# Issuing the loads of the backward phase from GpSimd, spreading a pair's and a group's pieces, and a last loop in two steps

## The chip, the cores and the metric

The kernel runs on one core of one Trainium2 chip. The core has a matrix engine (TensorE, PE in the profile, with its weight loads as PEld), VectorE (DVE), ScalarE (ACT), GpSimd (POOL) and SyncE (SP), which here only issues DMAs. All DMAs run on the core's 16 DMA engines. A DMA that SP or ACT issues goes through a hardware queue, one that POOL issues through a software queue; the profile lists these queues apart. The metric is the time of one execution on the device in microseconds; before and after are compared by the median of several runs.

## The reference

The kernel computes a transformer block whose attention and feed-forward halves stand side by side, and all its gradients:

```
def _A_ref(x, wqkv, wo):                       # attention, 16 heads of 28
    q, k, v = split((x @ wqkv))
    p = softmax(einsum("bhqd,bhkd->bhqk", q, k) * 28 ** -0.5)
    return einsum("bhqk,bhkd->bhqd", p, v) @ wo

def _B_ref(x, w_gate, w_up, w_down):           # SwiGLU, F = 1792
    return (silu(x @ w_gate) * (x @ w_up)) @ w_down

xn = layernorm(x)
out = x + _A_ref(xn, ...) + _B_ref(xn, ...)
outputs: out, and the vjp of it at grad_out for x, wqkv, wo, w_gate, w_up, w_down
```

x is [1, 2048, 448] in bf16. The 2048 rows are 16 tiles of 128.

## The kernel before

There are three stages. The **forward stage** (up to about 655 us of the span) runs attention forward, the feed-forward part forward and its weight gradients, and leaves in DRAM what later stages need: q, k, v and dO by columns (`qT_d`, `kT_d`, `vT_d`, `dOT_d`), the same by rows (`spq_d`, `spk_d`, `spo_d`), and chunks of hidden activations (`hd_d`).

The **backward stage** (about 656 to 1486 us) is one loop over 512 units and a short drain. The 16 heads are 4 groups of 4, a group is 2 pairs of heads, so there are 8 pairs. A unit is one pair, one block of 512 keys and one tile of 128 queries; 8 units make a window, 8 windows a pair, 16 windows a group, 64 windows the loop. In the code k counts the units, `W = k // 8` the windows and `pos = k % 8` the place in a window. A unit does this:

- PE: scores into PSUM (L852), dP into PSUM (L863); ACT: `E = exp(scores)` (L870); DVE: `ds = dP * E` (L881) into one of 8 buffers.
- six of the 8 `ds` tiles of a window are transposed by a DMA that SP issues (L883), the other two by PE (L776) with a copy by DVE or ACT (L783); all go into `dsT`, from which PE makes dq two windows later (L796).
- PE accumulates dK and dV from `ds` and `E` three units later (L749); every two windows ACT copies them out (`dkv_o`, L755), SP transposes them (L762) and POOL stores them (L764).

Beside the units every window carries one job on PE, given by the list `jobs`: windows 1 to 16 a row tile of the output (`y`, 18 chunk matmuls and x), windows 22 to 37, 42 to 49 and 55 to 62 a row tile of one half of the feed-forward part of dx (`dx`, 14 matmuls), windows 18 to 21, 38 to 41 and 51 to 54 a part of the gradient of wqkv (`dwq`); windows 0, 17, 50 and 63 have none. ACT copies a job's result out (`row_o`, L728) and POOL stores it (L730, L732).

What the backward stage reads comes by loads in the order in which the code issues them, on the queue of the issuing engine, which works through its instructions in order and stops at one whose semaphore is not there yet:

- `job_load` (L655) loads a job's chunk `ck` (448 or 576 KB) and, for `y`, a tile `x_c` (112 KB), two windows ahead, at `pos == 0`; three buffers.
- `load_pair` (L545) makes 8 pieces of 128 KB for the next pair: q and k in rows 0 to 63, dO and v in rows 64 to 127 of the tiles `qT` and `kT`, each in two halves of columns. They wait in the list `pload`.
- `load_group` (L558) makes 6 pieces of 256 KB for the next group (`v_sp`, `vT`, `O_sp`), in the list `gload`.
- `load_w` (L532) makes 7 pieces of a weight of 1568 KB or 2 of `wq`, in `wload`.

At `pos == 4` of each window the first 2 of `pload`, 1 of `gload` and 2 of `wload` are issued. All loads but that of `wd` are issued by SP, in one queue with the transposes. The first pair and the first group are loaded at the end of the forward stage.

The **last stage** (from 1494 us) is a loop over the 16 row tiles: PE sums dx through the projections (L957, L959), ACT copies it with a row sum (`g_sb`, `s1`, L963), DVE takes a product sum (`junk`, `s2`, L966), then `bb` (L970) and `cc` (L972); ACT makes `t1` (L975), DVE `t2` (L977), POOL adds the residual gradient (`dx`, L980) and SP stores it (L981).

Of the kernel before, what the change touches and what calls it, by code (L numbers as in the profile page):

```python
# [10 lines left out]
ALU = mybir.AluOpType  # L11
AX = mybir.AxisListType
FP32 = mybir.dt.float32
BF16 = mybir.dt.bfloat16
# [4 lines left out]
D = 448  # L19
# [3 lines left out]
G = 4  # L23
HP = 32
P = 128
NT = S // P
NFC = F // P
# [10 lines left out]
def kernel(  # L38
# [19 lines left out]
    pe, act, dve, pool, sp = nc.tensor, nc.scalar, nc.vector, nc.gpsimd, nc.sync  # L58
    ctx.enter_context(tc.manual_schedule())
    x_d = A_x.rearrange("b (t p) d -> p (b t) d", p=P)  # L60
    dy_d = grad_out.rearrange("b (t p) d -> p (b t) d", p=P)
    out0_d = out_0.rearrange("b (t p) d -> p (b t) d", p=P)
    out1_d = out_1.rearrange("b (t p) d -> p (b t) d", p=P)
# [9 lines left out]
    hd_d = dram.tile([NT, P, G + 3 * NFC, P], BF16, name="hd_d")  # L73
# [14 lines left out]
    xn_sp = const.tile([P, NT, DP], BF16, name="xn_sp")  # L88
# [39 lines left out]
    for b in (2, 3):  # L128
# [10 lines left out]
        out=r_ones[:], in_=ident_f[:].rearrange("p (a b) -> p a b", b=HP)[:, :, 28:30],  # L139
# [291 lines left out]
    for fc in range(NFC):  # L431
        nxt = dW_items(fc)
# [99 lines left out]
    def load_w(nm, parts):  # L532

        t = wp.tile([P, NFC, D], BF16, name="W")
        src = {"wd": B_w_down.rearrange("(fc p) d -> p fc d", p=P), "wg": wT_d[0], "wu": wT_d[1], "wq": wqT_d}[nm]
        n = 3 * G if nm == "wq" else NFC
        wtile[nm] = t
        step = n // parts
        q = pool if nm == "wd" else sp
        out = [lambda i=i: q.dma_start(out=t[:, i:i + step, :], in_=src[:, i:i + step, :])  # L540
               for i in range(0, n, step)]
        return out

# [2 lines left out]
    def load_pair(pr, parts):  # L546

        g, r = pr // 2, 64 * (pr % 2)
        q = qkp.tile([P, S], BF16, name="qT")
        k = qkp.tile([P, S], BF16, name="kT")  # L550
        qd[pr] = (q, k)
        n = S // parts
        return [lambda i=i, dst=dst, r0=r0, src=src: sp.dma_start(
                    out=dst[r0:r0 + 64, i:i + n], in_=src[g, r:r + 64, i:i + n])
                for r0, srcs in ((0, (qT_d, kT_d)), (64, (dOT_d, vT_d)))
                for dst, src in zip((q, k), srcs) for i in range(0, S, n)]

    def load_group(g, parts, kpool):  # L558

        spt[g] = [qkp.tile([P, NT, P], BF16, name="v_sp"), kpool.tile([P, S], BF16, name="vT"),  # L560
                  qkp.tile([P, NT, P], BF16, name="O_sp")]
        spt[g][1] = spt[g][1][:].rearrange("p (t c) -> p t c", c=P)
        n = NT // parts
        return [lambda i=i, t=t, src=src: sp.dma_start(
                    out=t[:, i:i + n, :].rearrange("p t c -> p (t c)"), in_=src[g, :, i * P:(i + n) * P])
                for t, src in zip(spt[g], (spq_d, spk_d, spo_d)) for i in range(0, NT, n)]

# [20 lines left out]
    for i, (g, qc, kt) in enumerate(steps):  # L588
# [25 lines left out]
        if i in (6, 8, 10, 12):  # L614
            j = i // 2 - 3
# [39 lines left out]
    def job_load(i):  # L655
        if i >= len(jobs) or jobs[i] is None:
            return
        j = jobs[i]
        if j[0] == "y":
            t = ckp.tile([P, NFC + G, P], BF16, name="ck")  # L660
            sp.dma_start(out=t[:], in_=hd_d[j[1], :, :G + NFC, :])
            x = ckp.tile([P, D], BF16, name="x_c")
            sp.dma_start(out=x[:], in_=x_d[:, j[1], :])
            chunk[i] = (t, x)
        elif j[0] == "dx":
            t = ckp.tile([P, NFC + G, P], BF16, name="ck")
            sp.dma_start(out=t[:, :NFC], in_=hd_d[j[2], :, G + NFC * (1 + j[1]):G + NFC * (2 + j[1]), :])
            chunk[i] = t

    def dwq_mms(g, c, ps):  # L670
# [160 lines left out]
    for k in range(N + 2 * UW):  # L831
        W, pos = k // UW, k % UW
        if k < N:
            pr, kc, w, qi = units[k]
            if k % 64 == 3 and pr + 1 < NPR:
                pload.extend(load_pair(pr + 1, 2))
            if k % 128 == 3 and pr + 2 < NPR:
                gload.extend(load_group(pr // 2 + 1, 2, vp if pr // 2 % 2 else ksp))
            if pos == 0:
                job_load(W + 2)  # L840
            if pos == 4:
                if W == len(jobs) - 1:
                    wload.extend(load_w("wq", 2))
                for lst, n in ((pload, 2), (gload, 1), (wload, 2)):
                    for f in lst[:n]:
                        f()
                    del lst[:n]
            q, kv = qd[pr]
            qt = 8 * w + qi
            s_ps = ps_sd.tile([P, 2, 512], FP32, name="sd")  # L850
            for j in range(2):
                pe.matmul(s_ps[:, j, :], lhsT=q[HP * j:HP * j + HP, qt * P:(qt + 1) * P],  # L852
                          rhs=kv[HP * j:HP * j + HP, kc * 512:(kc + 1) * 512],
                          start=True, stop=True, tile_position=(HP * j, 0))
        late_tr = pos == 0 and 1 <= W <= NW
        if 1 <= k <= N:
            pr, kc, w, qi = units[k - 1]
            q, kv = qd[pr]
            qt = 8 * w + qi
            d_ps = ps_sd.tile([P, 2, 512], FP32, name="sd")  # L860
            for j in range(2):
                r = 64 + HP * j
                pe.matmul(d_ps[:, j, :], lhsT=q[r:r + HP, qt * P:(qt + 1) * P],  # L863
                          rhs=kv[r:r + HP, kc * 512:(kc + 1) * 512],
                          start=True, stop=True, tile_position=(r, 0))
        if late_tr:
            pe_transpose(W - 1, TQ[1])
        if k < N:
            E[k] = ework.tile([P, 2, 512], BF16, name="E")
            act.activation(out=E[k][:], in_=s_ps[:], func=ACT.Exp, scale=SCALE)  # L870
        if late_tr:
            tr_out(act)
        job = jobs[W] if W < len(jobs) else None
        if pos == 6 and 2 <= W <= NW + 1:
            dq_out(W - 2)
        if 1 <= k <= N:
            if qi == 0:
                st[("dsT", (k - 1) // UW)] = twin.tile([P, 2, 4, UW * P], BF16, name="dsT")
            dsT = st[("dsT", (k - 1) // UW)]
            DS[k - 1] = dsw.tile([P, 2, 512], BF16, name="ds")  # L880
            dve.tensor_tensor(out=DS[k - 1][:], in0=d_ps[:], in1=E[k - 1][:], op=ALU.mult)  # L881
            if qi not in TQ:
                sp.dma_start_transpose(out=dsT[:, :, :, qi * P:(qi + 1) * P].rearrange("p j c q -> p (j c) q"),  # L883
                                       in_=DS[k - 1][:].rearrange("p j c -> p (j c)"))
        while sp_later:
            sp_later.pop(0)()

        if pos == 1:
            if 3 <= k < N + 3:
                acc_mm(k - 3)  # L890
            if job:
                st["aux"] = ps_x.tile([P, 512], FP32, name="aux")
                fillers = job_mms(W, st["aux"])
        if 1 <= pos < 5 and job:
            n = -(-len(fillers) // (5 - pos))
            for f in fillers[:n]:
                f()
            fillers = fillers[n:]
        if k == N + UW + 5:
            for c in range(4):  # L900
                if c % 2 == 0:
                    g_t = ps_sd.tile([P, 2, 512], FP32, name="sd")
                last_dwq.append((g_t[:, c % 2, :], dwq_mms(3, c, g_t[:, c % 2, :])))
            for _, m in last_dwq:
                for f in m[0][:12]:
                    f()
        if pos == 5 and 2 <= W <= NW + 1:
            dq_mm(W - 2, 0)
            dq_mm(W - 2, 1)
        if pos != 1 and 3 <= k < N + 3:  # L910
            acc_mm(k - 3)
        if pos == 4 and job:
            job_out(W, st["aux"])
        if pos == 6 and W < NW:
            pe_transpose(W, TQ[0])
            tr_out(dve)
# [5 lines left out]
    with ExitStack() as fin:  # L922
# [20 lines left out]
        for part in range(2):  # L943
            for c, (ps, m) in enumerate(last_dwq):
                for f in m[part][12 * (1 - part):]:
                    f()
                if part == 1:
                    dwq_out(3, c, ps)
        wq = wtile["wq"]
        for t in range(NT):  # L950
            if t % 2 == 0:
                load_c(t // 2 + 3, act)
# [5 lines left out]
            for n in range(3 * G):  # L958
# [14 lines left out]
                                     op0=ALU.mult, op1=ALU.mult)  # L973
            t1 = wk.tile([P, D], FP32, name="t1")
            act.activation(out=t1[:], in_=g_ps, func=ACT.Identity, scale=rstd[:, t:t + 1], bias=bb[:, 0:1])  # L975
            t2 = wk.tile([P, D], FP32, name="t2")
            dve.scalar_tensor_tensor(out=t2[:], in0=xn_sp[:, t, :D], scalar=cc[:, 0:1], in1=t1[:],  # L977
                                     op0=ALU.mult, op1=ALU.add)
            dx = wk.tile([P, D], BF16, name="dx")
            pool.tensor_tensor(out=dx[:], in0=t2[:], in1=dy_t[:, t, :], op=ALU.add)  # L980
            sp.dma_start(out=out1_d[:, t, :], in_=dx[:])  # L981
    cst.close()


# [28 lines left out]
```

## Time and profile before

| what | value |
|---|---|
| median of 3 runs (lowest, highest) | 1548.89 us (1547.53, 1555.15) |
| profiled execution, its span | 1549.43 us, 1547.7 us |
| busy PE, DVE, ACT, POOL | 1412.8, 1099.4, 1187.9, 396.1 us |
| backward stage, 656 to 1486 us: PE, DVE, ACT, POOL | 756.6, 678.7, 621.1, 110.1 us of 830.0 |
| its DMA rate, mean | 199 GB/s |
| transposes of `ds`: number, issue by SP (least, median, most) | 384, 1.231, 1.293, 5.001 us |

The span is the time from the first to the last instruction of the profiled execution; the execution itself was 1.8 us longer. A DMA's row on an issuing engine is the time that the issue takes; the data land later. Views used below: the page, the sums by window of time, the timeline of one engine in a stretch of time, and the chain of waits, which goes back from the last instruction by what released each.

### The profile page before, as it was taken

Reading aid. Unit: us, or ns where it says so; the run is one execution under the profiler, and the core shown is the slowest. Engines: PE = TensorE matmul, PEld = TensorE weight load, DVE = VectorE, ACT = ScalarE, POOL = GpSimd, SP = SyncE. Lnnn points to the kernel's source line nnn. Section 1 sums busy time; section 2 is a strip of 40 time slices with the busy share of each in tenths; the row PEclk is TensorE's granted clock in tenths of the full one; section 3 lists DMA queues with packets and bytes.
Section 4 is the critical chain, followed back from the end, with each engine's and each line's share of the span. In section 5 each row is a group of like instructions: output and inputs, shape, how many; then the busy total and the mean of one; then the engine's idle time right before and its main releaser. Section 6 shows DMA issues by size and latency. Waiting matters only on the chain.

```text
span 1547.7 us, 32024 instructions
## 1 busy us (share of the span) xinstructions
PE 1412.8 (91%) x12176; PEld 597.7 (39%) x12176; DVE 1099.4 (71%) x1421; ACT 1187.9 (77%) x1333; POOL 396.1 (26%) x664
## 2 busy tenths in 40 slices
PE   6899999999999989988988988989999889999987
PEld 3333333333333333433433444433335333543353
DVE  7654555656666657476877877878878789888935
ACT  6898988888788878676767867878778778888724
POOL 4341433343435355310110111111102101111033
PEclk9999999999999999999999999999999999999999
DMA  9985758767978689799999999999999999999994
GB/s 225 189 174 113 157 101 173 161 142 141 179 154 164 148 173 215 159 205 200 214 204 206 196 199 205 198 200 198 207 197 197 200 192 197 174 192 215 188 274 142
DMA packets 682106, 285.12 MB, mean 184 GB/s; under 512 B 637136, under 2 KB 650464, under 8 KB 681952
## 3 DMA queue, kind: packets, MB, share of 16 engines
q1 hardware_dynamic: 652016, 210.03, 74.6%
q0 software_dynamic: 25968, 64.53, 16.8%
q10 hardware_dynamic: 3968, 8.52, 1.6%
q8 instruction: 95, 1.56, 0.4%
q14 instruction: 59, 0.48, 0.1%
HBM read 67.34 MB, written 63.44 MB: 85 GB/s over the span
## 4 chain that ended last, share of the span: by engine, by line
PE 56%; DMA 13%; ACT 13%; DVE 8%; issue 6%; SPq 1%; POOL 1%; ACTq 0%; DVEq 0%; POOLq 0%
DMA dsT<-ds 9%; PE f_ps L357 7%; PE sd L852 6%; PE s_ps L600 6%; PE f_ps L383 6%; ACT E L870 5%; PE aux L719 4%; PE acc L749 4%; PE aux L796 4%; PE aux L776 4%; PE o_ps L582 4%; ACT eT L605 4%; DVE ds L881 3%; ACT dsT L783 3%; PE aux L713 3%
## 5 line engine op out<-in xcount | busy, mean ns | idle before, releaser
L881 DVE TENSOR_TENSOR ds<-sd,E 128x1024 bf16<-128x1024 f32 x512 | 611.4, 1220 | 137.5 <-DMA dsT<-ds 52.6
L870 ACT ACTIVATE E<-sd 128x1024 bf16<-128x1024 f32 x512 | 516.9, 1024 | 178.4 <-PE sd L863 140.2
L605 ACT ACTIVATE eT<-s_ps 128x1024 bf16<-128x1024 f32 x512 | 495.8, 1026 | 93.1 <-PE s_ps L600 89.6
L852 PE MATMUL sd<-kT,qT 32*128 32x512 bf16 x1024 | 201.8, 390 | 24.7 <-DVE ds L881 22.3
L863 PE MATMUL sd<-kT,qT 32*128 32x512 bf16 x1024 | 202.6, 389 | 23.6 <-ACT E L870 22.7
L749 PE MATMUL acc<-ds,v_sp 128*32 128x512 bf16 x1024 | 204.6, 395 | 0.7 <-DVE ds L881 0.7
L749 PE MATMUL acc<-E,O_sp 128*32 128x512 bf16 x1024 | 204.3, 395 | 0.2 <-ACT dkv_o L755 0.2
L600 PE MATMUL s_ps<-qT,kT 32*128 32x512 bf16 x1024 | 148.0, 386 | 7.8 <-ACT eT L605 5.6
L422 POOL DMA_DIRECT2D hd_d<-fT x168 | 126.9, 769 | 15.5 <-DVE fT L407 6.8
L383 PE MATMUL f_ps<-xnT,wgu 128*128 128x512 bf16 x448 | 118.8, 383 | 4.9 <-DVE w_sb L409 4.7
L764 POOL DMA_DIRECT2D dqkv_d<-dkv_o x64 | 39.3, 619 | 289.1 <-ACT dkv_o L755 287.3
L719 PE MATMUL aux<-W,ck 128*128 128x448 bf16 x448 | 108.4, 359 | 3.4
L852 PEld LDWEIGHTS <-qT 32*128 32x128 bf16 x1024 | 51.3, 91 | 154.1 <-issue 145.5
L582 PE MATMUL o_ps<-eT,v_sp 128*32 128x512 bf16 x1024 | 103.4, 394 | 0.6
L357 PE MATMUL f_ps<-xn_sp,f_sp 128*128 128x448 bf16 x448 | 99.1, 354 | 0.0
L749 PEld LDWEIGHTS <-O_sp 128*32 128x32 bf16 x1024 | 50.4, 94 | 113.4 <-issue 103.4
L600 PEld LDWEIGHTS <-kT 32*128 32x128 bf16 x1024 | 40.7, 91 | 137.7 <-issue 132.7
L776 PE MATMUL aux<-ident_bf,ds 128*128 128x128 bf16 x1024 | 79.4, 221 | 11.2 <-DVE dq_acc L808 5.8
L863 PEld LDWEIGHTS <-qT 32*128 32x128 bf16 x1024 | 65.4, 91 | 62.1 <-issue 58.2
L357 PEld LDWEIGHTS <-f_sp 128*128 128x128 bf16 x672 | 58.2, 98 | 77.4 <-issue 23.4
L776 PEld LDWEIGHTS <-ds 128*128 128x128 bf16 x1024 | 61.8, 98 | 39.8 <-issue 39.4
L395 DVE SCALAR_TENSOR_TENSOR g<-t_sb,f_ps 128x512 f32<-128x512 f32 x56 | 38.4, 686 | 53.3 <-ACT t_sb L393 53.2
(133 smaller groups left out, 1766.5 us busy)
## 6 DMA issues: line engine op xcount, KB each, us to landing
hd_d<-fT POOLq DMA_DIRECT2D x168, 128.0 KB, 4.4
ck<-hd_d SPq DMA_DIRECT2D x32, 448.0 KB, 4.4
ck<-hd_d SPq DMA_DIRECT2D x16, 576.0 KB, 5.1
dsT<-ds SPq DMA_TRANSPOSE x384, 4.2
dqkv_d<-dkv_o POOLq DMA_DIRECT2D x64, 64.0 KB, 3.8
dq_c<-dqkv_d ACTq DMA_DIRECT2D x5, 768.0 KB, 6.5
W<-wT_d SPq DMA_DIRECT2D x14, 224.0 KB, 3.6
out_dram<-dw_o POOLq DMA_DIRECT2D x28, 96.0 KB, 4.0
```

The source lines that it names most:

```text
L357: pe.matmul(acc[:, :D], lhsT=src[:, 12 * (t // 4) + 4 * wi + t % 4, :], rhs=rhs[:, t, :D], start=(t == 0), stop=(t == NT - 1))
L383: pe.matmul(st[name][:], lhsT=w(c), rhs=src[:, tsl, c, :], start=(c == 0), stop=(c == 3))
L582: pe.matmul(o_ps[HP * hh:HP * (hh + 1), :], lhsT=v[:, kt, HP * hh:HP * (hh + 1)], rhs=e[hh // 2][:, hh % 2, :], start=(kt == 0), stop=(kt ...
L600: pe.matmul(s_ps[:, j, :], lhsT=kT[r:r + HP, kt * P:(kt + 1) * P], rhs=qT[r:r + HP, qc * 512:(qc + 1) * 512], start=True, stop=True, tile_ ...
L605: act.activation(out=e[:], in_=s_ps[:], func=ACT.Exp, scale=SCALE)
L719: return [lambda n=n: pe.matmul(ps[:, :D], lhsT=t[:, n, :], rhs=w[:, n, :], start=(n == 0), stop=(n == NFC - 1)) for n in range(NFC)]
L749: pe.matmul(acc[r:r + HP, :], lhsT=src[:, qt, 64 * hp + HP * j:64 * hp + HP * j + HP], rhs=m[:, j, :], start=(qt == 0), stop=(qt == NT - 1 ...
L776: pe.transpose(ps[:, i, :], ds[:, i // 4, (i % 4) * P:(i % 4 + 1) * P], ident_bf[:])
L852: pe.matmul(s_ps[:, j, :], lhsT=q[HP * j:HP * j + HP, qt * P:(qt + 1) * P], rhs=kv[HP * j:HP * j + HP, kc * 512:(kc + 1) * 512], start=Tru ...
L863: pe.matmul(d_ps[:, j, :], lhsT=q[r:r + HP, qt * P:(qt + 1) * P], rhs=kv[r:r + HP, kc * 512:(kc + 1) * 512], start=True, stop=True, tile_p ...
L870: act.activation(out=E[k][:], in_=s_ps[:], func=ACT.Exp, scale=SCALE)
L881: dve.tensor_tensor(out=DS[k - 1][:], in0=d_ps[:], in1=E[k - 1][:], op=ALU.mult)
```

## The change

All loads of `load_w`, `load_pair`, `load_group` and `job_load` are issued by POOL instead of SP (the `wd` load was already). SP keeps the DMA transposes and, in the last stage, its loads and stores there. Of a pair's 8 pieces one is issued in each window instead of two, first halves of the columns first; of a group's 6 pieces one in every second window. In the last loop the second half of a tile's work (`t2`, `dx`, the store) is put behind the first half of the next tile, and the add of the last three tiles moves from POOL to DVE.

```
@@ load_w
-        q = pool if nm == "wd" else sp
-        out = [lambda i=i: q.dma_start(out=t[:, i:i + step, :], in_=src[:, i:i + step, :])
+        out = [lambda i=i: pool.dma_start(out=t[:, i:i + step, :], in_=src[:, i:i + step, :])
@@ load_pair
-        return [lambda i=i, dst=dst, r0=r0, src=src: sp.dma_start(
+        return [lambda i=i, dst=dst, r0=r0, src=src: pool.dma_start(
@@ load_group
-        return [lambda i=i, t=t, src=src: sp.dma_start(
+        return [lambda i=i, t=t, src=src: pool.dma_start(
@@ job_load
-            sp.dma_start(out=t[:], in_=hd_d[j[1], :, :G + NFC, :])
+            pool.dma_start(out=t[:], in_=hd_d[j[1], :, :G + NFC, :])
-            sp.dma_start(out=x[:], in_=x_d[:, j[1], :])
+            pool.dma_start(out=x[:], in_=x_d[:, j[1], :])
-            sp.dma_start(out=t[:, :NFC], in_=hd_d[j[2], :, G + NFC * (1 + j[1]):G + NFC * (2 + j[1]), :])
+            pool.dma_start(out=t[:, :NFC], in_=hd_d[j[2], :, G + NFC * (1 + j[1]):G + NFC * (2 + j[1]), :])
@@ loop over units
             if k % 64 == 3 and pr + 1 < NPR:
-                pload.extend(load_pair(pr + 1, 2))
+                nxt = load_pair(pr + 1, 2)
+                pload.extend(nxt[0::2] + nxt[1::2])
-                for lst, n in ((pload, 2), (gload, 1), (wload, 2)):
+                for lst, n in ((pload, 1), (gload, W % 2), (wload, 2)):
@@ last loop
+        def finish(t, t1, cc):
+            t2 = wk.tile([P, D], FP32, name="t2")
+            dve.scalar_tensor_tensor(out=t2[:], in0=xn_sp[:, t, :D], scalar=cc[:, 0:1], in1=t1[:],
+                                     op0=ALU.mult, op1=ALU.add)
+            dx = wk.tile([P, D], BF16, name="dx")
+            add = pool if t < NT - 3 else dve
+            add.tensor_tensor(out=dx[:], in0=t2[:], in1=dy_t[:, t, :], op=ALU.add)
+            sp.dma_start(out=out1_d[:, t, :], in_=dx[:])
...
             act.activation(out=t1[:], in_=g_ps, func=ACT.Identity, scale=rstd[:, t:t + 1], bias=bb[:, 0:1])
-            t2 = wk.tile([P, D], FP32, name="t2")
-            dve.scalar_tensor_tensor(out=t2[:], in0=xn_sp[:, t, :D], scalar=cc[:, 0:1], in1=t1[:],
-                                     op0=ALU.mult, op1=ALU.add)
-            dx = wk.tile([P, D], BF16, name="dx")
-            pool.tensor_tensor(out=dx[:], in0=t2[:], in1=dy_t[:, t, :], op=ALU.add)
-            sp.dma_start(out=out1_d[:, t, :], in_=dx[:])
+            if t > 0:
+                finish(t - 1, *held)
+            held = (t1, cc)
+        finish(NT - 1, *held)
```

## The prediction

> **What bounds the kernel now.** I started with the page: its span, the chain that ended last and the costliest group. The profiled execution took 1549.43 us, 0.5 above the median of 1548.89, for a span of 1547.7 us; the sum below is made against it.
>
> ```profile
> span 1547.7 us, 32024 instructions
> ...
> DMA dsT<-ds 9%; PE f_ps L357 7%; PE sd L852 6%; PE s_ps L600 6%; PE f_ps L383 6%; ACT E L870 5%; PE aux L719 4%; PE acc L749 4%; PE aux L796 4%; PE aux L776 4%; PE o_ps L582 4%; ACT eT L605 4%; DVE ds L881 3%; ACT dsT L783 3%; PE aux L713 3%
> ...
> L881 DVE TENSOR_TENSOR ds<-sd,E 128x1024 bf16<-128x1024 f32 x512 | 611.4, 1220 | 137.5 <-DMA dsT<-ds 52.6 <-PE sd L863 51.5 <-ACT E L870 13.5
> ```
>
> The longest single item of the chain is a transfer, the transposes of `ds`, and DVE, which makes `ds`, loses 52.6 us waiting for them: `ds` has 8 buffers, so its tile k needs the transpose of tile k-8 to be done. All this is in the backward phase. Its 512 `ds` instructions run from 658.0 to 1473.4 us, 815.4 us; I cut that into its 64 windows of 8 units and asked for L881 window by window (columns: stretch, length, DVE busy, TensorE clock, DMA share, GB/s).
>
> ```profile
> core 0: us, DVE busy (x), PEclk, DMA share, GB/s
> 714.60:729.90 15.30, 9.53 (x9) 1.00 1.05 203
> 729.90:741.70 11.80, 9.41 (x9) 1.00 1.15 237
> ...
> 896.50:913.70 17.20, 9.64 (x9) 0.90 1.01 199
> 1090.50:1102.40 11.90, 9.67 (x10) 1.00 1.10 224
> 1130.60:1145.00 14.40, 9.65 (x10) 0.86 1.02 195
> ...
> 1366.30:1378.10 11.80, 9.62 (x10) 1.00 1.08 195
> ```
>
> The work of a window is the same, yet its length goes from 11.8 to 17.2 us. After 1366 us, where the last pair's loads are over, all are 11.8 to 12.1. The long ones move fewer GB/s than the short ones, so bytes alone don't stretch them. Then SP's own rows inside the window of 14.4 us (start, us, line):
>
> ```profile
> 1128.21 1.26 SPq L883 DMA_TRANSPOSE dsT<-ds  x1
> 1129.53 1.22 SPq L553 DMA_DIRECT2D kT<-vT_d  x2
> 1130.79 0.58 SPq L564 DMA_DIRECT2D vT<-spk_d  x1
> 1131.48 9.64 SPq L883 DMA_TRANSPOSE dsT<-ds  x6
> 1141.20 1.23 SPq L762 DMA_TRANSPOSE dkv_sp<-dkv_o  x1
> 1142.49 0.58 SPq L564 DMA_DIRECT2D O_sp<-spo_d  x1
> 1143.17 6.76 SPq L883 DMA_TRANSPOSE dsT<-ds  x5
> ```
>
> SP issues back to back for 21.7 us with 0.05 us between rows. **The bound of the stretched windows is SP's issue time.** From the records of all SP rows between 658.0 and 1473.4: 428 transposes 652.7 us (mean 1.525), 152 loads 95.2 us (0.63 each), 580 gaps of 0.06: 783 of 815 us. The median transpose is 1.29 us; the excess of the mean, (1.525 - 1.29) x 428 = 101 us, is 0.66 us for each load, for transposes that stand right behind loads in the ring are issued slowly (up to 2.8 us). So a window's SP time is 6.75 transposes x 1.35 = 9.1 us, plus 1.35 us for each load (0.63 + 0.06 + 0.66). Test on groups: windows 1 to 16 have 3.2 loads each, 13.4 us by this, and measure 13.5; windows 18 to 21 have 3.75, 14.2, and measure 14.4; windows 55 to 62 have 1.1, 10.6, and measure 11.9, the pitch that the compute engines set.
>
> **The change part by part.**
>
> *Loads from SP to POOL.* SP loses all 152 loads and keeps 9.1 us of transposes a window plus whatever surcharge s loads in another queue still put on them. If s stays 0.66, a `y` window (3.4 loads after the change) costs SP 9.1 + 2.2 = 11.3 and the others (2.1 loads) 10.5, both below the compute pitch. The pitch comes from windows with little SP lag: 11.91 for `dx` (mean of 55 to 62), 12.0 for `dwq` (51 to 54), 10.8 and 10.9 for those without a job, and 12.2 for `y` (mean of 5 to 7 and 13 to 16). Gains: `y` 216.0 - 16 x 12.2 = 20.8; `dwq` 155.5 - 144.0 = 11.5; first `dx` 203.6 - 190.6 = 13.0; `dx` 42 to 49 99.7 - 95.3 = 4.4; sum 49.7. I leave 4 us of it for `y` windows in which loads and transposes still meet (windows 6 and 7 took 12.5 and 12.7), and take 46. Bounds: all `y` at 11.9 gives 54; nothing gained if s rises (rivals).
>
> *POOL's side.* 152 issues more. A load has no POOL row of this shape; the stores L732 (0.57) and L764 (0.62), and 1.10 for the 1568 KB `W` load of L540, bound one by 0.5 and 1.1 us; I take 0.6, near the plain stores: 3.4 x 0.6 + 1.2 = 3.3 us of a 12 us window, where POOL's busy time is now 0.6 to 3.0. POOL is in order, so a load waits behind a `row_o` store that waits for ACT (up to 15.6 us) or a `dkv_o` one (18.4). That costs nothing while chunk i is asked for two windows (24 us) ahead, landing in 4.4 to 5.1, and pair pieces at least three units ahead. If that cover went, PE would wait for its next chunk or `qT` by what is late, some us per pair, 7 times. The first chunk loses most cover: SP issues it at 657.3, POOL only after its stores end at 662.5; landing 5.5 us later is 668.0, and the first `ck` weights load at 669.4. Zero, with 0 to 3 us for the range. The 7 loads of the first pair and group (578 to 606 us) join a POOL with waits of its own in a stretch that PE bounds: zero.
>
> *Pieces spread.* One pair piece a window instead of two in four of eight, a group piece every second window: no instruction more or less. It flattens the load, and its worth is inside the 46. The last piece of a pair is issued in the eighth window, about 4 units (6 us) before the next pair, and needed later still, since it holds the second half of the columns; landing 3.0 to 3.5 us covers it.
>
> *Tail in two steps.* In the last loop a tile's pieces chain: ACT `t1`, DVE `t2`, POOL `dx`, and the next `bb` on DVE ends only with `dx`:
>
> ```profile
> 1540.51 0.69 DVE L977 SCALAR_TENSOR_TENSOR t<-xn_sp,cc,t 128x448 f32<-128x448 bf16 x1 [0.85 <-ACT t L975]
> 1541.66 0.67 DVE L970 SCALAR_TENSOR_TENSOR bb<-s,rstd 128x1 f32<-128x1 f32 x1
> ...
> 1541.28 1.03 POOL L980 TENSOR_TENSOR dx<-t,dy_t 128x448 bf16<-128x448 f32 x1 [1.70 <-DVE t L977]
> ```
>
> `bb` takes 0.67 where its first two took 0.16, and the tile's period is 2.73 us against 2.65 for PE alone (the pitch of the first tiles). Moving `t2` and `dx` behind the next tile's `cc` breaks the ring: PE ends at 1494.1 + 16 x 2.65 = 1536.5 instead of 1537.8. Then g_sb 0.75, junk 0.7, bb and cc 0.3, `t2` of tile 14 0.69, its add on DVE, `t2` of tile 15 0.69, its add. No DVE add of this shape is in the trace; L881's 1.19 ns per element gives 0.53, L508's 1.35 gives 0.61; I take 0.6. That ends at 1540.9; now POOL's last `dx` ends at 1545.0. Gain 4.1, say 4, bounds 1 (if a wait for loads holds PE's pitch) and 5.
>
> The Trainium skill has the reason for the slow `bb`: "SBUF — State Buffer", section "Who interferes with whom", says that a DVE instruction with two SBUF inputs shuts out, or is shut out by, a GpSimd instruction that reads SBUF. The trace agrees, 0.67 against 0.16 us; by the rule the `t2` moved next to another `dx` could be blocked for up to 1.0 us too, which PE's 2.65 us would hide.
>
> **Sum.** 1549.4 - 46 - 4 = 1499 us.
>
> **The rivals.**
> 1. *Transposes still held in `y` windows.* If s is 1.2, a `y` window is 9.1 + 3.4 x 1.2 = 13.2, 1 us over the pitch, others 11.6, under it: 1499 + 16 = 1515. For it: a `y` window would move 2.9 MB (transposes 1.77, chunk 0.59, the rest 0.55), 244 GB/s at 11.9 us, over any full window's (237). Against: 224 and 237 at full pitch.
> 2. *The DMA engines bind, whoever issues.* Then 162.4 MB at the mean of 199 GB/s is 816 us as now, and the tail alone is left: 1545. The skill says so in general: "DMA: Bandwidth & Descriptors", section "Issuing engines are not separate DMA queues", has it that several issuing engines save only the sequencer's time, usually small beside the DMA. Here 783 of 815 us of SP's time is not small. Against it too: 224 GB/s and more in windows of 12 us.
> 3. *Slower: POOL's packets in a queue of their own cut into the transposes.* With SP bound everywhere the windows sum to 591 + 145 x s us (54 for 16 `y` windows, 91 for 44 others); from s = 1.57 that beats the gain of the tail and it is slower; at 1.8 it is 852, and 1582 us in all. For it: from 606 to 617 us POOL issued some 10 stores, and a transpose of `fT` beside them took 4.25 us where the median is 1.46, the next on SP 3.48 instead of 1.47. Against: these 4.8 us are 0.5 a store, below 0.66.
> 4. *The change doesn't do what it says*, loads late behind POOL's waits: the cover above, some 5 us on a gain of 50; its chance is counted with the forecast, whose range holds it.
>
> **Chances.** Forecast 0.70 (own range 1487 to 1508), first rival 0.14, second 0.07, third 0.09. The range 1487 to 1530 takes in the forecast and the first rival. A measurement of this kernel tells 0.5% (7.7 us) from no change: faster 0.84, same 0.07, slower 0.09.
>
> **What would show it.** Right: SP rows with idle time between transposes, no DVE wait for `dsT<-ds` near 52.6 us, `y` windows at 12.2 to 12.4, `dwq` and `dx` at 12, clock 1.00 throughout, POOL's load rows near 0.6 us; in the tail `bb` at 0.16 and a period of 2.65. Wrong: mean transpose issue above 1.7 us, windows of 14 us without SP lag, or PE waiting for `ck`, `qT` or `kT`.

## The result and the profile after

| kernel | median of its runs, us (lowest, highest) | ratio to before, 95% interval |
|---|---|---|
| before | 1548.21 (1545.40, 1555.15) | |
| after | 1615.97 (1606.34, 1622.29) | 1.0425 [1.0353, 1.0498] |

The change makes the kernel 4.2% slower; 1499 us had been forecast. Medians here and below are of all runs of a kernel, ratios of those within 1.5% of its fastest run. The profiled execution of the changed kernel took 1610.19 us. First the page of the changed kernel: span, chain by line, and the group of `ds`.

```profile
span 1608.4 us, 32018 instructions
...
DMA dsT<-ds 17%; PE f_ps L357 7%; PE f_ps L383 6%; PE s_ps L599 6%; PE sd L852 5%; ACT eT L604 4%; PE acc L748 4%; PE aux L795 4%; PE aux L718 4%; ACT E L870 4%; PE o_ps L581 3%; PE aux L775 3%; PE aux L712 2%; DVE ds L881 2%; PE sd L969 2%
L881 DVE TENSOR_TENSOR ds<-sd,E 128x1024 bf16<-128x1024 f32 x512 | 610.5, 1219 | 197.9 <-DMA dsT<-ds 126.4
```

DVE's own work is what it was (610.5 us), but it now waits 126.4 us for transposes of `ds`, 73.8 more than before, and their share of the chain went from 9 to 17%. The 512 units run from 658.7 to 1538.3 us: 879.6 us against 815.4, so 64.2 us are lost there. The first `ds` comes 0.7 us later than before, and from the end of the last to the end of the span it is 70.1 us where it was 74.3, so 4.2 us come back there; the span grew by 60.7. The cut of L881 by windows (stretch, length, DVE busy, TensorE clock, DMA share, GB/s):

```profile
core 0: us, DVE busy (x), PEclk, DMA share, GB/s
694.00:706.50 12.50, 9.52 (x9) 1.00 0.96 191
732.50:753.00 20.50, 9.39 (x9) 0.83 1.14 169
790.60:809.70 19.10, 9.60 (x10) 0.82 1.15 190
...
931.60:953.40 21.80, 9.50 (x8) 0.92 1.21 157
1102.40:1114.20 11.80, 9.61 (x10) 1.00 1.12 183
```

The loss isn't spread evenly. 46 of the 64 windows last 12.17 us on average, close to the pitch that was forecast (769.4 / 64 = 12.0). The other 18 are longer than 14 us and take 319.8 us, 17.8 each; before there were 13 such windows with 193.2 us. The windows of 20.5 and 21.8 us move 169 and 157 GB/s at a DMA share of 1.14 and 1.21, the one of 11.8 us 183 at 1.12: the DMA engines are as busy with packets and move less.

How a long window comes about is seen on POOL and SP just ahead of the one of 21.8 us (start, us, engine, line; idle time ahead in brackets):

```profile
921.95 1.20 POOL L763 DMA_DIRECT2D dqkv_d<-dkv_o  x2 [8.90 <-ACT dkv_o L754]
923.13 0.54 POOL L552 DMA_DIRECT2D qT<-dOT_d  x1
923.67 1.10 POOL L539 DMA_DIRECT2D W<-wT_d  x2
924.76 1.07 POOL L698 COPY dwq_z<-dwq_raw 128x56 bf16<-128x56 bf16 x6
926.12 0.72 POOL L699 DMA_DIRECT2D out_dram<-dwq_z  x1 [0.30 <-POOL dwq_z L698]
926.73 0.65 POOL L552 DMA_DIRECT2D kT<-vT_d  x1
927.27 0.65 POOL L563 DMA_DIRECT2D v_sp<-spq_d  x1
927.83 1.15 POOL L539 DMA_DIRECT2D W<-wT_d  x2
```

POOL stood 8.90 us before a store that waits for ACT. Everything queued behind it, two pieces of a pair, one of a group and four of weights, then leaves with three stores in 7 us. SP in the same time:

```profile
918.73 1.28 SPq L817 DMA_TRANSPOSE dq_sp<-dq_o  x1
920.10 7.73 SPq L883 DMA_TRANSPOSE dsT<-ds  x4
927.92 1.65 SPq L761 DMA_TRANSPOSE dkv_sp<-dkv_o  x1
929.66 3.07 SPq L883 DMA_TRANSPOSE dsT<-ds  x1
```

Four transposes take SP 7.73 us, where four of 1.29 would take 5.2; those issued at 916 to 918 us landed 3.3 us later, those issued from 922.9 to 929.7 landed 8.6 to 10.0 us later. Over the whole stage the transposes of `ds` land 5.47 us after their issue (4.30 before), 63 of them later than 8 us (none before). SP's 428 transposes take 1.871 us each against 1.525, so SP, rid of 95 us of loads, needs 148 us more for transposes; its gaps of over 0.3 us sum to 36 of the 880 us.

The longest window is the first, 22.8 us where it was 11.8. POOL issues nine loads in it from 663.00 to 668.08 us, right behind its stores; the first two transposes land 16.0 and 15.5 us after their issue, and DVE stands:

```profile
681.48 3.49 DVE L881 TENSOR_TENSOR ds<-sd,E 128x1024 bf16<-128x1024 f32 x3 [11.63 <-DMA dsT<-ds]
```

In the last stage `bb` takes 0.15 us and the period is 2.65 us, (1602.97 - 1592.38) / 4:

```profile
1592.38 0.15 DVE L980 SCALAR_TENSOR_TENSOR bb<-s,rstd 128x1 f32<-128x1 f32 x1
...
1602.97 0.15 DVE L980 SCALAR_TENSOR_TENSOR bb<-s,rstd 128x1 f32<-128x1 f32 x1
```

### The profile page after: what moved, and what is told of

Same layout as the page of the kernel before. It is cut to its first block, busy times and chain, and to the rows that moved or that the text cites. A ratio compares the mean times of both kernels' runs of the same rounds, so it can differ in the third digit from the quotient of the medians.

```text
span 1608.4 us, 32018 instructions
## 1 busy us (share of the span) xinstructions
PE 1430.6 (89%) x12176; PEld 598.7 (37%) x12176; DVE 1094.6 (68%) x1424; ACT 1189.1 (74%) x1333; POOL 479.4 (30%) x822
## 4 chain that ended last, share of the span: by engine, by line
PE 55%; DMA 21%; ACT 11%; DVE 7%; issue 6%; POOL 1%; SPq 0%; DVEq 0%; ACTq 0%; POOLq 0%
DMA dsT<-ds 17%; PE f_ps L357 7%; PE f_ps L383 6%; PE s_ps L599 6%; PE sd L852 5%; ACT eT L604 4%; PE acc L748 4%; PE aux L795 4%; PE aux L718 4%; ACT E L870 4%; PE o_ps L581 3%; PE aux L775 3%; PE aux L712 2%; DVE ds L881 2%; PE sd L969 2%
## 5 line engine op out<-in xcount | busy, mean ns | idle before, releaser
L881 DVE TENSOR_TENSOR ds<-sd,E 128x1024 bf16<-128x1024 f32 x512 | 610.5, 1219 | 197.9 <-DMA dsT<-ds 126.4
L852 PE MATMUL sd<-kT,qT 32*128 32x512 bf16 x1024 | 206.9, 400 | 83.8 <-DVE ds L881 81.8
L863 PE MATMUL sd<-kT,qT 32*128 32x512 bf16 x1024 | 207.6, 398 | 22.0 <-ACT E L870 21.3
L748 PE MATMUL acc<-ds,v_sp 128*32 128x512 bf16 x1024 | 208.7, 403 | 0.7 <-DVE ds L881 0.7
L748 PE MATMUL acc<-E,O_sp 128*32 128x512 bf16 x1024 | 208.5, 403 | 0.2 <-ACT dkv_o L754 0.2
L795 PE MATMUL aux<-dsT,vT 128*32 128x512 bf16 x1024 | 81.9, 428 | 0.4
```

The costliest lines, as they stand in the source:

```text
L748: pe.matmul(acc[r:r + HP, :], lhsT=src[:, qt, 64 * hp + HP * j:64 * hp + HP * j + HP], rhs=m[:, j, :], start=(qt == 0), stop=(qt == NT - 1 ...
L795: pe.matmul(ps[r:r + HP, :], lhsT=Ks[:, kc * 4 + kt, 64 * hp + HP * j:64 * hp + HP * j + HP], rhs=dsT[:, j, kt, s_ * 512:(s_ + 1) * 512], ...
```

## The experiments

All twelve kernels are timed against the kernel before. "Harm" below is the time above that of the kernel with every load on SP and the two other parts of the change (the second experiment, 1540.07 us).

### The last loop alone

The kernel before with nothing but `finish` and `held` from the diff.

> The kernel before with the last loop in two steps alone. Every theory of the loads leaves this run alone: the last stage should lose the 2.73 us ring and end about 4 us earlier, 1544 to 1545 us against 1548.5, ratio 0.997. If the changed kernel's loss had its place in the last loop, it would be slower than before.

1545.43 us (1538.82 to 1553.01), ratio 0.9982 [0.9963, 1.0001]; the 64 windows sum to 816.0 us (815.4 before). From the last `ds` to the end of the span it is 71.1 us instead of 74.3, a gain of some 3 us; the interval of the ratio just takes in no change.

### Everything but the queue

```
-        out = [lambda i=i: pool.dma_start(out=t[:, i:i + step, :], in_=src[:, i:i + step, :])
+        q = pool if nm == "wd" else sp
+        out = [lambda i=i: q.dma_start(out=t[:, i:i + step, :], in_=src[:, i:i + step, :])
...
-            pool.dma_start(out=t[:], in_=hd_d[j[1], :, :G + NFC, :])
+            sp.dma_start(out=t[:], in_=hd_d[j[1], :, :G + NFC, :])
```

The same in `load_pair`, `load_group` and for the other loads of `job_load`.

> All loads stay on SP, pieces spread over the windows, last loop in two steps. Theory 1 (copies in a queue other than that of the transposes cut into them packet by packet) and theory 2 (only POOL's software queue does) both expect no loss here: SP stays at its 9.1 us of transposes plus 1.35 us a load, but no window has more than 4 loads, so 1525 to 1543 us. Theory 3 (the new order of the pieces, or pieces that come late, is what costs) expects this slow as well, 1580 us or more.

1540.07 us (1536.30 to 1544.61), ratio 0.9947 [0.9929, 0.9965]. So the spread of the pieces is worth some 5 us on SP (windows 808.6 instead of 816.0), and the move to POOL alone costs 1615.97 - 1540.07 = 76 us.

### The same loads from ACT's hardware queue

The changed kernel with `act` in place of `pool` in the five loads.

> The changed kernel with the loads issued by ACT, in ACT's hardware queue, instead of POOL. Theory 1 (any second queue cuts into the transposes): as slow as the changed kernel, 1590 us or more, transposes with issues of 3 to 8 us and landings above 8 us. Theory 2 (POOL's software queue alone): SP is free and nothing cuts into the transposes, 1500 to 1520 us, median landing of the transposes 4 us or less; ACT pays 0.4 us a load.

1549.80 us (1544.92 to 1558.74), ratio 1.0012 [0.9988, 1.0036]: the time of neither theory, but the transposes tell "any second queue" from "POOL's queue". From the waits of DVE in the stage (us, times, longest):

```profile
DVE ds L882 <- PE sd L864: 86.5, 198, 0.9
...
DVE ds L882 <- DMA dsT<-ds: 1.4, 1, 1.4
```

and from the DMA issues of its page (KB, median us to landing):

```profile
ck<-hd_d ACTq DMA_DIRECT2D x32, 448.0 KB, 4.1
...
dsT<-ds SPq DMA_TRANSPOSE x384, 4.4
```

The wait for transposes is gone (1.4 us), SP stands idle for 117 us, and a transpose takes SP 1.545 us: the surcharge is (1.545 - 1.29) x 428 / 152 = 0.72 us a load, about the 0.66 that the forecast used. What the forecast said of SP is true of a second hardware queue. The time doesn't fall, for ACT now issues the loads between its own instructions: of the `dx` windows, 55 to 59, in each of which ACT issues a chunk, take 12.52 or 12.79 us where they took 11.78 or 12.05, and window 61, in which it issues nothing, takes 11.78 as before. `ds` waits for dP (86.5 us, 51.5 before) instead of transposes.

### POOL without the spreading

```
-                pload.extend(nxt[0::2] + nxt[1::2])
+                pload.extend(load_pair(pr + 1, 2))
...
-                for lst, n in ((pload, 1), (gload, W % 2), (wload, 2)):
+                for lst, n in ((pload, 2), (gload, 1), (wload, 2)):
```

> The changed kernel with the pieces as before, two of a pair and one of a group in a window. Theories 1 and 2: as slow as the changed kernel or slower, since two pieces and a chunk then meet in one window, 1605 to 1640 us. Theory 3 (the spreading costs): back to 1550 us or less.

1620.81 us (1610.91 to 1634.22), ratio 1.0473 [1.0427, 1.0520]: 4.8 us above the changed kernel, but the runs overlap, and in its profile the windows sum to 873.2 us against 879.6. With the loads on POOL no worth of the spreading is shown; it isn't what does the harm.

### Half of the loads on POOL

First only `ck` and `x_c` on POOL, then only pairs, groups and weights, the rest on SP.

> The changed kernel with only the chunks ck and x_c (64 loads, 25 MB) on POOL; pairs, groups and weights (88 loads, 17 MB) on SP. Theory 1 (a load in POOL's software queue reaches the 16 DMA engines at different times and breaks the step that the transposes need, for as long as its bytes last): loss over e2_sp_spread by bytes, 60% of 76 us, about 1585 us, transposes with landings over 8 us beside chunks alone. Theory 2 (the number of loads in the queue counts): 42%, about 1572. Theory 3 (only all of it together saturates something, POOL or its ring): near e2, 1530 to 1545.

> The other half: pairs, groups and weights on POOL, the chunks on SP. Theory 1: 40% of the loss, about 1570 us, and windows 55 to 62, which have no such loads, at 11.9 us. Theory 2: 58%, about 1584. Theory 3: 1530 to 1545.

Chunks alone: 1564.66 us (1562.25 to 1568.40), ratio 1.0101 [1.0070, 1.0132], harm 24.6 us. The others alone: 1551.18 us (1539.60 to 1564.33), ratio 1.0012 [0.9980, 1.0044], harm 11.1 us (8.5 without the two longest of its ten runs); its one profile is of an execution 11.6 us above that median, so nothing is read from it. Both expectations by bytes or by number missed, and in the same direction: 24.6 + 11.1 = 36 us at the most, not 76. More than half of the harm is there only when both kinds come from POOL.

### Fewer loads, or none, in SP's ring

Two tests of the forecast's other half, that SP's issue time is the bound and that windows fall to a pitch of 12 when it is lifted. In the first the loads are larger and fewer (105 instead of 152: a pair in 4 pieces, a group in 3, a weight in 2), all on SP; in the second the chunk loads are left out.

> e2_sp_spread with larger and fewer loads on SP: a pair in 4 pieces of 256 KB, a group in 3 of 512 KB, a weight in 2 of 784 KB, one at a time in alternate windows; 105 loads instead of 152, the same bytes. If SP's issue time bounds the stretched windows and a load costs it 0.69 us itself, 47 x 0.69 = 32 us of SP time are saved in the 40 windows that have them: 1515 to 1530 us. If the bytes in the ring are what costs (the 0.66 us of surcharge and more), no faster than e2: 1538 to 1548.

> e2_sp_spread in which the first chunk ck and x_c are used by all jobs: 62 loads (24 MB) are left out, all matmuls stay. If SP's issue time bounded the stretched windows, SP falls to 9.1 + 1.4 x 1.35 = 11.0 us a window, under the pitch of the compute engines, and the 64 windows take what the prediction took for them, 765 to 775 us instead of 809: 1497 to 1507 us. If that pitch was wrong (the compute engines need more than 12 us), windows stay above 780 us and the time above 1512.

Fewer loads: 1532.39 us (1528.24 to 1534.80), ratio 0.9894 [0.9871, 0.9917], 7.7 us better than the same with 152 loads, but 2.4 us above the range that was expected for it. Without chunk loads: 1507.42 us (1504.53 to 1509.44), ratio 0.9735 [0.9709, 0.9762], 0.4 us above its range, and no window is longer than 13.7 us. A `y` and a `dx` window of the latter, in the columns used above:

```profile
747.70:760.20 12.50, 9.61 (x10) 1.00 0.85 169
1088.80:1100.60 11.80, 9.61 (x10) 1.00 1.12 198
```

The waits of its DVE:

```profile
DVE ds L888 <- PE sd L870: 61.9, 149, 1.7
...
DVE ds L888 <- DMA dsT<-ds: 0.5, 1, 0.5
```

With 62 loads fewer on SP its transposes no longer hold anything up (0.5 us), and the windows sum to 777.3 (765 to 775 were expected). That fits the bound as it was named, and the pitch, but for `y`: 12.5 instead of 12.2. The run takes 25 MB off the DMA engines too, though, so by itself it doesn't tell SP's issue time from their bytes; the copies below do.

### Copies in place of transposes

Two theories for the harm. One: a transpose needs all 16 DMA engines in step, and POOL's loads reach the engines at different times and break the step. The other: POOL's queue holds up whatever SP issues. For them the transposes of `ds` are replaced by plain copies of the same size:

```
-                sp.dma_start_transpose(out=dsT[:, :, :, qi * P:(qi + 1) * P].rearrange("p j c q -> p (j c) q"),
-                                       in_=DS[k - 1][:].rearrange("p j c -> p (j c)"))
+                sp.dma_start(out=dsT[:, :, :, qi * P:(qi + 1) * P],
+                             in_=DS[k - 1][:].rearrange("p j (c q) -> p j c q", q=P))
```

once in the changed kernel, once in the kernel with all loads on SP.

> The changed kernel with the 384 DMA transposes of ds replaced by plain DMA copies of the same bytes in pieces of 256 B, same queue, same waits (dsT then holds ds untransposed, so dq is another quantity). Theory 1 (a transpose needs all 16 DMA engines in step, and POOL's loads take them out of it): the harm goes with the transposes; copies land in 3 to 6 us, none beside a POOL load over 8 us, and the time is as in e10_copy_sp or below it, 1490 to 1520 us. Theory 2 (POOL's software queue takes the DMA engines' time from whatever SP has queued): still 50 us or more above e10_copy_sp, copies landing after 8 to 16 us.

> e2_sp_spread with the same replacement: the partner of e9_copy_pool. Both theories: at or below e2's 1540 us, 1500 to 1540, depending on what SP pays to issue a copy in pieces of 256 B.

Loads on POOL: 1518.12 us (1514.01 to 1524.63), ratio 0.9793 [0.9750, 0.9836]. Loads on SP: 1504.40 us (1503.35 to 1506.55), ratio 0.9704 [0.9672, 0.9735]. The harm of POOL's queue falls from 76 to 13.7 us. From the two pages, POOL's first (KB, us to landing):

```profile
dsT<-ds SPq DMA_DIRECT2D x384, 256.0 KB, 5.0
```

```profile
dsT<-ds SPq DMA_DIRECT2D x384, 256.0 KB, 4.5
```

But the first theory expected no copy to land later than 8 us, and 35 did (2 with the loads on SP); the mean landing rises by 0.8 us (4.61 to 5.43), that of transposes by 1.2 (4.32 to 5.47). So POOL's queue delays copies too. Part of the difference in time may be SP's slack: a copy takes it 0.60 us to issue (median), a transpose 1.29, and with all loads on SP it has 256 us of idle time to catch up with copies, 22 with transposes. Neither theory stands alone.

The run with the loads on SP also answers the prediction's second rival. Its windows move the same 162.4 MB in 769.2 us, 211 GB/s, so a mean of 199 GB/s was not a limit of the DMA engines for these bytes.

### The best of what was learnt

Fewer, larger loads; `ck`, pairs and `wq` on SP, `x_c`, later groups and the two other weights on ACT; the last loop in two steps.

> e7_sp_big with x_c, the groups and two weights issued by ACT, 29 loads; 76 stay on SP. SP saves 29 x 1.35 = 39 us, ACT pays 0.35 to 0.45 us for each, 12 us in all: windows 1 to 16 at 12.5 instead of 12.9, 18 to 21 at 12.4 instead of 13.0, so 1520 to 1528 us. If a second hardware queue harms the transposes too, or ACT's waits cost more than its issues, 1532 us or more.

1527.77 us (1525.10 to 1533.69), ratio 0.9857 [0.9828, 0.9886]: the fastest kernel here that computes everything, 1.4% below the kernel before.

### POOL's loads spaced out

The halves add up to 36 us and the whole is 76; both long windows looked at above begin where POOL's loads come late and leave in a burst. So the changed kernel was run with POOL held back:

```
+    def pace(k):
+        if k:
+            pc = outp.tile([P, 1], BF16, name="pace")
+            pool.tensor_copy(out=pc[:], in_=E[k - 1][:, 0, 0:1])
...
             if pos == 0:
+                pace(k)
                 job_load(W + 2)
...
-                for lst, n in ((pload, 1), (gload, W % 2), (wload, 2)):
-                    for f in lst[:n]:
-                        f()
-                    del lst[:n]
+                due = [(pload, 1)]
+            if pos == 2:
+                due = [(wload, 1)]
+            if pos == 6:
+                due = [(gload, W % 2), (wload, 1)]
+            for lst, n in due:
+                for f in lst[:n]:
+                    pace(k)
+                    f()
+                del lst[:n]
```

> The changed kernel with POOL paced: in a unit POOL issues the first chunk at position 0, then, before each further load, copies one column of the E tile that ScalarE has made for the position before (so the copy waits for that moment of the unit): a weight piece at position 2, a pair's piece at position 4, a group's piece at position 6. Same loads, same queue, same bytes; only that they no longer leave POOL within one or two us of each other. If the harm is one price per load (each load from POOL's queue delays the transposes by itself, whatever else is in flight), the time stays at 1605 to 1616 us, the windows sum near 875, and some 55 to 63 of 432 transposes still land later than 8 us. If it is the bunching of POOL's loads that makes 76 us out of the 25 and 11 us that the chunks alone and the other loads alone cost over the kernel with every load on SP (1540), the time falls to about the sum of the two, 1575 us, or below it, the windows sum to about 843, and the landings over 8 us to under 30.

1548.25 us (1533.98 to 1571.19; 1545.04 without the two longest of its ten runs), ratio 0.9971 [0.9940, 1.0003]: 68 of the 76 us are gone, with the same loads, bytes and queue. Its profiled execution took 1562.93 us; 14 us of its excess lie ahead of the first `ds` (673.1 instead of 658.7), so its backward stage can be read: windows 816.2 us, 9 of them over 14 us. POOL there, around a window of that place, and the group of `ds` on its page:

```profile
934.39 0.19 POOL L828 COPY pace<-E 128x1 bf16<-128x1 bf16 x1 [2.20 <-ACT E L883]
934.83 0.54 POOL L552 DMA_DIRECT2D kT<-vT_d  x1 [0.26 <-issue]
...
940.08 0.19 POOL L828 COPY pace<-E 128x1 bf16<-128x1 bf16 x1 [0.73 <-ACT E L883]
940.53 0.54 POOL L666 DMA_DIRECT2D ck<-hd_d  x1 [0.26 <-issue]
```

```profile
L894 DVE TENSOR_TENSOR ds<-sd,E 128x1024 bf16<-128x1024 f32 x512 | 610.9, 1220 | 136.9 <-DMA dsT<-ds 55.5
```

The wait for transposes is back at 55.5 us (52.6 before the change, 126.4 after it). In the changed kernel 74 of 154 loads are issued within 1 us of the one before, in this one 22; three or more loads are in flight for 160 us there and 43 here (41 in the kernel before, 21 with all on SP and spread, 98 with only the chunks on POOL). Sorted by the most loads that were in flight at one moment between their issue and landing, the transposes of `ds` land alike in the two kernels (with two loads 6.08 and 5.91 us on average, with three 6.84 and 7.08; before the change 4.60 and 4.17), but 49 of 384 meet four or more in the changed kernel and 6 in the paced one. A longer flight meets more loads too, so this sorting alone doesn't tell cause from effect; the paced run does that. "One price per load" falls: it asked for 1605 us or more. A price per load remains, though: transposes still take SP 1.734 us, a surcharge of (1.734 - 1.29) x 428 / 152 = 1.25 us, and 30 land later than 8 us, where the bunching theory wanted fewer. What SP saves on the loads it gives back in slower transposes, 742 us for them instead of 653 for transposes and 95 for loads, and the time is that of the kernel before. Pacing also fixes the place in the unit at which a load leaves; that was not told apart from the distance between loads.

## Why the prediction was wrong

**The bound: right.** SP's issue time held the long windows. Loads taken away from SP and not put on POOL shortened the windows: 47 loads fewer, for the same bytes, by 12.9 us (808.6 to 795.7), 62 chunk loads left out by 31.3, to 777.3, near the pitch. Copies, which cost SP half as much to issue as transposes, brought them to 769.2 with all bytes and loads in place. But "1.35 us for each load" is no price per load in its second half: with 105 larger loads the surcharge on the transposes is (1.554 - 1.29) x 427 = 113 us, with 152 it is (1.513 - 1.29) x 427 = 95. By these two runs it goes with the bytes rather than with the number, and fewer loads save the 0.69 us of issue and gap alone, 47 x 0.69 = 32, of which 113 - 95 = 18 are given back; the 14 that are left are near the 12.9 measured. Nor does it need a load ahead in SP's ring, as the forecast read it: with the loads in ACT's queue it was there all the same (0.72). And the slowest issue of a transpose behind loads took 5.0 us before the change, not 2.8.

**The pitch: right but for `y`.** With SP out of the way (copies, loads on SP) the windows sum to 769.2 us; the forecast had 815.4 - 46 = 769.4. `y` windows are 12.5 and not 12.2, 199.6 us for the 16 instead of 195.2, which the 4 us left for them cover; `dwq` and `dx` came out as forecast.

**Loads from SP to POOL: wrong, and this is the step that failed.** It said "If s stays 0.66" and took that. The surcharge of a load on the transposes is (1.871 - 1.29) x 428 / 152 = 1.64 us from POOL's queue. For ACT's hardware queue it is 0.72, so the step carried a number from one kind of queue to another. The forecast's own sign for it, a mean issue of a transpose above 1.7 us, was met with 1.871. The third rival, at 0.09, named what came, transposes slowed by POOL's queue, and the right sign. Its point of 1.57 was passed. What was held against it, 4.8 us for some 10 stores of the forward stage, 0.5 a store, was too small a measure: those were stores, most of 128 KB, beside two transposes, and the loads of the backward stage are up to 576 KB.

**The average hid the rest.** The rival's sum, 591 + 145 s, gives 829 us at 1.64, and 879.6 were measured. The sum gives every window the same s. In the changed kernel 46 windows run near the pitch and 18 carry the loss, so what s takes above the mean in the loud ones is not paid back in the quiet ones.

**POOL's side at zero: wrong.** The price of an issue was right (0.54 to 0.67 us). The cover named, chunks two windows ahead, did hold for the data. The first chunk, for which 0 to 3 us were allowed, landed at 667.24, even ahead of the 668.0 forecast, yet its window lost 11.0 us, for with it left eight more loads. What goes late behind a store goes together: 8.9 us of standing still became a burst of 10 DMAs, and holding POOL's loads apart brought 68 us back.

**Pieces spread: right in sign on SP**, some 5 us there, for which the forecast had no figure of its own; on POOL no worth is shown. **Tail in two steps: right**, 3.2 us alone and 4.2 in the changed kernel where 4 were forecast (bounds 1 and 5), with `bb` at 0.15 us and the period at 2.65.

**The clock: not 1.00 throughout**, as the forecast asked, but 0.958 on average (0.978 before). It was 0.88 in the 18 long windows and 0.98 in the others; that it falls there because PE had stood idle fits, but no run tests it.

The Trainium skill, "DMA: Bandwidth & Descriptors", section "Issuing engines are not separate DMA queues", has all issuing engines' DMAs interleave on the same 16 engines and sees a saving of issue time only. For SP and ACT these runs agree (0.66 and 0.72 us a load). For POOL they don't: the same loads cost 76 us, and 68 of these went when the loads left at other moments.

What stays open is why a load from POOL's queue weighs more than one from a hardware queue. A burst isn't always needed: 12 of the 63 transposes that landed late never met more than one load at a time. One stretch of the changed kernel, in its window of 21.8 us, shows it bare, with a single chunk load (issued at 939.31, landed 12.66 us later) beside three transposes. From 943.3 us nothing else of POOL's is in flight, and DVE waits 5.71 us for a transpose that lands at 952.15 (columns as above):

```profile
core 0: us, DVE busy (x), PEclk, DMA share, GB/s
937.00:939.00 2.00, 0.11 (x1) 1.00 1.25 248
...
941.00:944.00 3.00, 2.46 (x4) 0.63 1.26 120
944.00:947.00 3.00, 2.57 (x3) 1.00 1.23 77
947.00:950.00 3.00, 0.00 (x0) 1.00 1.26 58
950.00:952.00 2.00, 0.00 (x0) 1.00 1.15 66
```

Ahead of it transposes alone move 284 to 289 GB/s in packets of 256 bytes that take 18 ns each. While the load is under way the rate falls to 58, and those packets take 54 to 406 ns (means of half microseconds, 944 to 951.5 us); of the load's own 64 packets none to seven start in each half microsecond. When the last has come, at 952 us, the rate is 284 GB/s again. The spread from the first to the last of the 16 engines to finish a chunk load fits: its 90th percentile is 5.61 us in the changed kernel, 1.44 in the one before and 0.77 with ACT's queue. Transposes that need the engines in step would suffer from such a spread, but no run shows that they do, and copies suffered too. Nor does any run take away the larger packets of POOL's loads (7168 bytes where the hardware queues have 3584), another difference between the queues.

The Trainium skill, "SBUF — State Buffer", section "Who interferes with whom", offers another reason: a DMA of GpSimd's queue starves while a VectorE instruction in a two-port mode keeps GpSimd from writing its descriptors, and a hardware queue is the remedy. The remedy agrees with the run on ACT's queue; the reason doesn't fit this stretch, where DVE was busy for 0.00 us from 947 to 952 and the rate stayed at 58 and 66 GB/s.

## What to carry to other kernels

A load's price need not go with it to another kind of queue: beside DMA transposes it was 0.66 us on SP, 0.72 on ACT's queue and 1.64 on POOL's here. Before loads are put behind an engine that waits for others, look at what leaves when it stops waiting; a burst can cost more than the same loads one by one, and holding them apart brought 68 of 76 us back here. And where an issuing engine is the bound, fewer and larger loads on it (152 to 105) gained 7.7 us, while moving all of them to another queue lost 9.7 us on ACT's and 76 on POOL's.

## What the runs showed that was not expected

A load in POOL's queue goes in packets of 7168 bytes, two rows of a chunk, where SP's and ACT's queues make packets of 3584. POOL's loads of 448 KB land 6.1 us after their issue in the changed kernel (median), against 4.4 on SP and 4.1 on ACT, though the issue of a chunk costs POOL no more than SP (0.56 us on average against 0.71, and 0.34 on ACT). And a transpose costs SP 1.29 us to issue, a copy of as many bytes 0.60.
